# Up projection of an mLSTM + GELU kernel: float32r products of 12-bit parts in place of summed fp32 blocks

## The chip, the cores and the metric

The kernel runs on one core of a Trainium2 chip. The metric is the device time of one execution in microseconds: 517.59 us before the change, the median of three runs (517.13 to 517.72). The profile is one execution of the program as the hardware profiler recorded it; its span from the first to the last instruction is 515.2 us.

## The reference

Two parts follow each other. The first is an mLSTM cell over 4 batches, 8 heads, 768 steps and head size 40, written as a recurrence over time:

```python
for t in range(S):
    m_new = np.maximum(f_gate[:, :, t] + m, i_gate[:, :, t])
    f_stab = np.exp(f_gate[:, :, t] + m - m_new)
    i_stab = np.exp(i_gate[:, :, t] - m_new)
    C = f_stab * C + i_stab * outer(v_t, k_t)
    n = f_stab * n + i_stab * k_t
    y[:, :, t] = sigmoid(o_gate_t) * (C @ q_t) / max(abs(n . q_t), 1)
```

The second takes x, which is y with the heads laid side by side (3072 tokens x 320), and computes `out = gelu(x @ w_in) @ w_out` with the exact gelu, w_in of 320 x 2048 and w_out of 2048 x 320. The two weights arrive as float64 and the result is float32, so x @ w_in has to be computed to about fp32's accuracy.

## The kernel before

**Stages.** The sequence is cut into six chunks of 128 steps; a chunk of all four batches is 512 tokens. For each chunk c and batch b a *cell* (n = 4c + b) turns q and k (`turn`, letter T), makes the decay weights (`mask` M, `weights` W), multiplies them by the scores (`scores` S), takes the part carried from earlier chunks (`carry` C), applies them to v (`values` V), divides (`finish` Y) and turns the result so that features lie on partitions (`turn_y`, X). When the four X of a chunk are done, its *up* (x @ w_in and gelu) can run, and then its *down* (times w_out). The down of chunk c is interleaved with the cells of chunk c + 1 by hand: the string FRONT gives the order for the start (cells of chunks 0 and 1, conversion of the weights from float64 in 26 pieces by K and J, the whole up and down of chunk 0 as A, U and F), and the string DOWN gives it for the down of every later chunk but the last; F is one step of the down, Z a piece of preparation for the weights. The order within an engine's queue is the order in which these letters are played. There are no planner's choices.

**Up before.** For chunks 1 to 5, `summed_up` (products at L597, rest at L626) computes the first 256 features of the contraction as a product of 2 x 2 blocks with seven block products instead of eight (Strassen's form, in Winograd's variant). Rows of x^T are one pair of blocks, halves of the 2048 columns the other, halves of the 512 tokens the third. Each block product is eight fp32 matmuls of 128 x 128 weights with 256 columns. It needs sums of weight blocks (`in_sum`, Z in FRONT, DVE), sums of x blocks (`sum_x`, L587, DVE), and sums of the products, which DVE makes from PSUM into the tile g (L608 to L612 and L639, 512 elements a partition). The remaining 64 features are plain products of half height (`rest`, L626), whose two halves use the two halves of TensorE's rows side by side. gelu follows on ACT (L637, L640), and `hidden_sums` (L525 to L527, DVE) forms the sums that the down needs, since the down too uses seven products (`down_steps`, L682).

**PSUM.** Eight banks in four pairs, with the tags tr, h, a and b. An up takes one bank of each pair for its four result blocks, so that two sets alternate.

**Cell data.** Each of q, k, v and the output gate has four buffers (NLD = 4) and is loaded for cell n + 4 after `turn_y` of cell n. The running maxima M of a cell, 512 KB spread over all partitions, come by DMA from a scratch tensor in memory into two tiles of their own (`Mb`, NM = 2); POOL masks them (L334), ACT makes the weights W from them (L359) in another four tiles. The 64 last features of y are doubled within the gate's tile (L460), so that the third transpose of `turn_y` (L470) yields them on both halves of the partitions.

Of the kernel before, what the change touches and what calls it, by code (L numbers as in the profile page):

```python
# [9 lines left out]
F32 = mybir.dt.float32  # L10
BF16 = mybir.dt.bfloat16
# [4 lines left out]
P = 128  # L16

I23 = 2.0 ** 23

# [6 lines left out]
    O0 L0 I1 I1 g0 E L1 P0 O2 P1 w0 t0 N D K w1 L2 P2 Q P3 s0 O1 t1 w2 L3 c0 J K v0 K s1 y0 w3 t2 I3 g1 v1 O3 I2 I3  # L26
    I5 J c1 B5 I2 K y1 I4 I2 s2 x0 O4 L4 t3 J x1 B4 s3 v2 I7 g3 L5 g2 c2 c3 y2 v3 x2 O5 L6 K J G0 A y3 x3 J H M0 M1
    K K J T0 W0 O6 M2 O7 A J W1 S0 C0 K J T1 L7 U U K Z K V0 T2 A M3 J J G1 S1 K W2 W3 K C1 Z A S2 Z V1 G2 J Y0 J K
    C2 Z T3 J K Y1 U U J S3 Z V2 C3 K J K K J J F K F F F Z J K J X0 K K J F F F Z J F K G3 Y2 F J K V3 J K F K X1 J
    J F F F F K Z X2 B8 J F Y3 X3 B9 F"""  # L30
DOWN = """
    M0 Z M1 T0 W0 F F T1 W1 Z G3 Z F S0 Z S1 C0 M2 Z C1 G1 G0 M3 V0 Y0 Z V1 W2 Z F F T2 W3 F T3 F G2 Z Y1 S2 S3 C2
# [4 lines left out]
def kernel(  # L37
# [19 lines left out]
    L = P  # L57
# [12 lines left out]
    NM = 2  # L70
    NB = 4
    WP = 512
    assert S % L == 0 and 3 * BH <= P and DFF % (4 * WP) == 0 and DM == NX * P + R and DM <= WP and D <= DP and NLD == B == 4

    const = ctx.enter_context(tc.tile_pool(name="const", bufs=1))
    wts = ctx.enter_context(tc.tile_pool(name="wts", bufs=B))
    raw = ctx.enter_context(tc.tile_pool(name="raw", bufs=2))
    two = ctx.enter_context(tc.tile_pool(name="two", bufs=2))
    outp = ctx.enter_context(tc.tile_pool(name="outp", bufs=2))
    dram = ctx.enter_context(tc.tile_pool(name="dram", bufs=1, space=bass.MemoryType.DRAM))  # L80
# [10 lines left out]

    w_in = const.tile([P, NX, 2, DFF // 2], F32, name="w_in")
    w_rest = const.tile([P, DFF // 2], F32, name="w_rest")
# [4 lines left out]
    xT = const.tile([P, NX + 1, TG], F32, name="xT")  # L98
# [5 lines left out]
    qb = [const.tile([P, H, DP], F32, name=f"qb{n}") for n in range(NLD)]  # L104
    kb = [const.tile([P, H, DP], F32, name=f"kb{n}") for n in range(NLD)]
    vb = [const.tile([P, H, D1], F32, name=f"vb{n}") for n in range(NLD)]

    ob = [const.tile([P, DM + R], F32, name=f"ob{n}") for n in range(NLD)]
# [7 lines left out]
    def out_of(n):  # L116
        return ob[n % NLD][:, 0:DM].rearrange("p (h d) -> p h d", d=D)

    def load(n, first=0, end=4):

        if n >= NCH * B:
            return
        c, b = divmod(n, B)
        for src, dst in ((q, qb), (k, kb), (v, vb), (o_gate, None))[first:end]:
            nc.sync.dma_start(out=dst[n % NLD][:, :, 0:D] if dst else out_of(n),
                              in_=src[b, :, c * L:(c + 1) * L, :].rearrange("h p d -> p h d"))
# [3 lines left out]
    def load_M(n):  # L130

        if n >= NCH * B:
            return
        c, b = divmod(n, B)
        Mb[n] = wts.tile([P, H, L], F32, name="Mb", tag="Mb", bufs=NM)
# [5 lines left out]
    for t in kb[0:B] + qb[0:B]:  # L141
        nc.gpsimd.memset(t[:, :, D:DP], 0.0)
    for t in vb[0:B]:
        nc.gpsimd.memset(t[:, :, D:D1], 1.0)
# [106 lines left out]
    for f in range(0, DFF // 2, WP // 2):  # L251
        for x in range(NX):
            pieces.append(([w_src["in"][x * P:(x + 1) * P, w_cols(e, f, WP // 2)] for e in range(2)],
                           w_in[:, x, :, f:f + WP // 2]))
        if f % WP == 0:
            pieces.append(([w_src["in"][NX * P:DM, w_cols(e, f, WP)] for e in range(2)], w_rest[:, f:f + WP]))
    n_in = len(pieces)
# [34 lines left out]
    def conv_two(i):  # L292

        if i < len(pieces):
# [5 lines left out]
            if len(dst.shape) == 3:  # L300
                s, p = [t.rearrange("p (e f) -> p e f", e=2) for t in (s, p)]
# [20 lines left out]
    class Cell:  # L322


        def __init__(self, c):
            self.c = c

            self.engine = nc.vector if c < 2 else nc.gpsimd
            self.qT, self.kT, self.vw, self.far, self.hs = {}, {}, {}, {}, {}
# [7 lines left out]
        def weights(self, b):  # L337

            n = self.c * B + b
            W[n] = wts.tile([P, H, L], F32, name="W", tag="W")  # L340
            if self.c > 0:
                M_n = Mb.pop(n)
# [17 lines left out]
            if self.c > 0 and not 2 * B <= n + NM < 2 * B + NM:  # L360
                load_M(n + NM)

        def gate(self, b):
            o = ob[(self.c * B + b) % NLD][:, 0:DM]
            nc.scalar.activation(out=o, in_=o, func=AF.Sigmoid)

        def turn(self, b):
            n = self.c * B + b
            for src, store, name in ((kb, self.kT, "kT"), (qb, self.qT, "qT")):
                pt = ps_tr.tile([P, NP, L], F32, name="pt", tag="tr")  # L370
                unread(pt[:, 0, :])
                for p in range(NP):
                    nc.tensor.transpose(pt[:, p, :], src[n % NLD][:, 2 * p:2 * p + 2, :].rearrange("p h d -> p (h d)"),  # L373
# [6 lines left out]
        def weigh_values(self, b):  # L380
            vw = self.vw[b] = two.tile([P, H, D1], F32, name="vw", tag="vw")
            self.engine.tensor_tensor(out=vw, in0=vb[(self.c * B + b) % NLD],
# [17 lines left out]
        def carry(self, b):  # L400
# [9 lines left out]
            if c + 1 < NCH:  # L410
                vw = self.vw.pop(b)
                for p in range(NP):
                    for hip in range(2):
                        nc.tensor.matmul(pc[halves[hip], p, :], kb[n % NLD][:, 2 * p + hip, :], vw[:, 2 * p + hip, :],  # L414
                                         start=True, stop=True)
            if c > 0:
# [4 lines left out]
                self.far[b] = two.tile([P, H, D1], F32, name="far", tag="far")  # L421
# [12 lines left out]

        def values(self, b):
# [6 lines left out]
            for h in range(H):  # L442
                for r in halves:
                    nc.tensor.matmul(ph[r, h, :], Pm[:, h, r], vb[n % NLD][:, h, :], start=True, stop=True)  # L444
# [3 lines left out]
            hs = self.hs[b] = two.tile([P, H, D1], F32, name="hs", tag="hs")  # L448
            nc.vector.tensor_tensor(out=hs, in0=ph, in1=self.far.pop(b), op=OP.add)

        def finish(self, b):
            n, hs = self.c * B + b, self.hs.pop(b)
            ys, y = ob[n % NLD], out_of(n)
            self.engine.tensor_tensor(out=y, in0=hs[:, :, 0:D], in1=y, op=OP.mult)
            den = two.tile([P, H], F32, name="den", tag="den")
# [343 lines left out]
```

## Time and profile before

| stretch of the span (us) | what runs | length | TensorE busy | DVE busy | ACT busy |
|---|---|---|---|---|---|
| 0 to 57.5 | cells of chunk 0, first weights | 57.5 | 45.9 | 46.0 | 43.6 |
| 57.5 to 96.0 | cells of chunk 1, up of chunk 0 | 38.5 | 38.4 | 33.0 | 36.1 |
| 96.0 to 133.2 | down of chunk 0, w_out converted | 37.2 | 37.2 | 32.7 | 18.3 |
| 133.2 to 164.9 | up of chunk 1 | 31.7 | 31.7 | 21.9 | 11.0 |
| 164.9 to 212.8 | down of chunk 1, cells of chunk 2 | 47.9 | 47.9 | 35.3 | 25.1 |
| 449.6 to 481.3 | up of chunk 5 | 31.7 | 31.7 | 18.7 | 10.5 |
| 481.3 to 515.2 | down of chunk 5 | 33.9 | 30.7 | 10.6 | 3.3 |

Chunks 2 to 4 repeat the two rows of chunk 1, with ups of 31.6 to 31.7 us. Over the whole span TensorE is busy for 500.3 us (97%), DVE for 340.2 (66%), ACT for 255.0 (49%) and POOL for 60.9 (12%). The granted TensorE clock is 0.992 of full speed on average. A busy engine in such a table need not be the bound: whether it is follows from which wait ends last in the stage, and for that the chain of waits has to be read.

### The profile page before, as it was taken

To read this page: it belongs to the slowest core of one execution; us is meant where nothing else is said; L and a number is where in the kernel's file an instruction comes from. 1 tells how busy PE (TensorE), PEld (TensorE's weight loads), DVE (VectorE), ACT (ScalarE), POOL (GpSimd) and SP (SyncE) were. 2 spreads that over 40 slices of the span, in tenths; PEclk is the share of its full clock that TensorE was granted. 3 is DMA by queue.
4 is the path that set the end of the run, shared out by engine and by line. 5 is a ranking of instruction groups with operands and counts; after the bars stand their busy time and mean duration, and the time that the engine had idled before them with its cause. 6 is when DMAs were issued, how large, how long until landed. Compare 5 with 4: busy or idle time off the path is not lost.

```text
span 515.2 us, 10957 instructions
## 1 busy us (share of the span) xinstructions
PE 500.3 (97%) x4472; PEld 450.6 (87%) x4472; DVE 340.2 (66%) x696; ACT 255.0 (49%) x523; POOL 60.9 (12%) x98
## 2 busy tenths in 40 slices
PE   4889999999999999999999999999999999999997
PEld 3778888767888999988999988999988999988997
DVE  7789598999577887347668347678347657237621
ACT  7696999555344960152980132982123882124300
POOL 3002100000210225000145000053000021000000
PEclk9799999999999999999999999999999999999999
DMA  6999751279900254900234900124920020000001
GB/s 128 223 214 212 184 147 53 64 163 171 198 0 1 84 116 58 167 0 2 74 88 69 167 28 1 43 83 81 166 52 2 5 80 1 27 27 0 1 2 51
DMA packets 111442, 41.62 MB, mean 81 GB/s; under 512 B 101184, under 2 KB 104416, under 8 KB 111392
## 3 DMA queue, kind: packets, MB, share of 16 engines
q1 hardware_dynamic: 111392, 40.92, 37.5%
q8 instruction: 35, 0.57, 0.5%
q14 instruction: 15, 0.12, 0.1%
HBM read 36.90 MB, written 4.01 MB: 79 GB/s over the span
## 4 chain that ended last, share of the span: by engine, by line
PE 91%; ACT 4%; DVE 3%; issue 0%; DMA 0%; SPq 0%; DVEq 0%; ACTq 0%
PE po L682 30%; PE pu L597 24%; PE pu L626 7%; PE po L659 7%; PE pu L538 5%; PE ps L395 4%; PE ph L444 4%; PE pt L373 4%; PE pf L419 2%; PE pf L414 2%; PE pu L544 1%; PE px L470 1%; ACT W L359 1%; ACT pow L285 1%; ACT pow L286 1%; DVE M L194 1%
## 5 line engine op out<-in xcount | busy, mean ns | idle before, releaser
L682 PE MATMUL po<-w_out,g 128*128 128x160 f32 x640 | 91.5, 299 | 0.0
L682 PEld LDWEIGHTS po<-w_out,g 128*128 128x128 f32 x640 | 88.0, 190 | 0.3 <-DVE g L639 0.3
L597 PE MATMUL pu<-xT,w_in 128*128 128x256 f32 x240 | 58.8, 381 | 0.0
L639 DVE TENSOR_TENSOR g<-pu,g 128x512 f32<-128x512 f32 x60 | 40.5, 689 | 22.4 <-PE pu L626 21.0
L597 PEld LDWEIGHTS pu<-xT,w_in 128*128 128x128 f32 x240 | 45.0, 190 | 7.5 <-ACT g L640 1.7
L471 ACT COPY xT<-px 128x384 f32<-128x384 f32 x24 | 11.1, 480 | 77.9 <-PE px L470 77.8
L359 ACT ACTIVATE W<-Mb,aT 128x128 f32<-128x128 f32 x160 | 48.9, 391 | 0.1
L682 PE MATMUL po<-w_sums,sums 128*128 128x160 f32 x320 | 47.3, 302 | 0.0
L398 DVE TENSOR_TENSOR W<-ps,W 128x512 f32<-128x512 f32 x48 | 30.2, 683 | 23.9 <-PE ps L395 21.2
L334 POOL TENSOR_SCALAR_AFFINE_SELECT Mb<-Mb 128x1024 f32<-128x1024 f32 x20 | 22.9, 1155 | 185.3 <-DMA Mb<-M_d 131.2
L682 PEld LDWEIGHTS po<-w_sums,sums 128*128 128x128 f32 x320 | 44.0, 190 | 0.4
L606 ACT COPY g<-pu 128x512 f32<-128x512 f32 x20 | 11.6, 582 | 58.2 <-PE pu L597 58.2
L695 DVE TENSOR_TENSOR o_sb<-po,o_sb 128x320 f32<-128x320 f32 (+1 forms) x27 | 12.5, 463 | 39.4 <-PE po L682 36.2
L637 ACT ACTIVATE g<-pu 128x512 f32<-128x512 f32 x20 | 12.0, 598 | 52.7 <-PE pu L626 52.7
L597 PE MATMUL pu<-x_sums,in_sums 128*128 128x256 f32 x160 | 37.8, 379 | 0.0
L626 PE MATMUL pu<-xT,w_rest 64*128 64x256 f32 x320 | 37.2, 382 | 0.0
L640 ACT ACTIVATE g<-g 128x512 f32<-128x512 f32 x60 | 36.1, 627 | 1.9
L608 DVE TENSOR_TENSOR g<-pu,g 128x512 f32<-128x512 f32 x20 | 13.8, 692 | 34.6 <-PE pu L597 28.8
L626 PEld LDWEIGHTS pu<-xT,w_rest 64*128 64x128 f32 x320 | 30.1, 187 | 6.4 <-issue 3.3
L659 PE MATMUL po<-w_out,g 128*128 128x320 f32 x128 | 35.7, 434 | 0.0
L597 PEld LDWEIGHTS pu<-x_sums,in_sums 128*128 128x128 f32 x160 | 30.2, 190 | 4.3
L659 PEld LDWEIGHTS po<-w_out,g 128*128 128x128 f32 x128 | 23.8, 190 | 9.3
(140 smaller groups left out, 884.3 us busy)
## 6 DMA issues: line engine op xcount, KB each, us to landing
Mb<-M_d SPq DMA_DIRECT2D x20, 512.0 KB, 3.7
bits<-in_moe_w_in_dram SPq DMA_DIRECT2D x20, 256.0 KB, 4.6
bits<-in_moe_w_out_dram SPq DMA_DIRECT2D x16, 320.0 KB, 3.0
vb<-in_v_dram SPq DMA_DIRECT2D x24, 160.0 KB, 4.9
ob<-in_o_gate_dram SPq DMA_DIRECT2D x24, 160.0 KB, 4.2
qb<-in_q_dram SPq DMA_DIRECT2D x24, 160.0 KB, 4.0
kb<-in_k_dram SPq DMA_DIRECT2D x24, 160.0 KB, 4.5
out_dram<-o_sb SPq DMA_DIRECT2D x24, 160.0 KB, 3.0
```

What stands on the lines that cost most here:

```text
L334: nc.gpsimd.affine_select(out=t, in_=t, compare_op=OP.is_ge, fill=1.0e30, base=0, pattern=[[0, H], [1, L]], channel_multiplier=-1)
L359: nc.scalar.activation(out=W[n][:, h, :], in_=src, func=AF.Exp, scale=-1.0, bias=aT[:, self.c, r:r + 1])
L373: nc.tensor.transpose(pt[:, p, :], src[n % NLD][:, 2 * p:2 * p + 2, :].rearrange("p h d -> p (h d)"), ident)
L395: nc.tensor.matmul(ps[hip][:, p, :], kT[r, p, :], qT[r, p, :], start=True, stop=True)
L398: nc.vector.tensor_tensor(out=w, in0=ps[hip], in1=w, op=OP.mult)
L538: nc.tensor.matmul(banks[-1][e][:, i - i0, :], w_in[:, x, e, i * P:(i + 1) * P], xT[:, x, t0:t1], start=(x == 0 and i == i0), stop=False, ...
L597: nc.tensor.matmul(to[:, j, :], lhs[:, (f0 + j) * P:(f0 + j + 1) * P], rhs, start=(first and j == 0), stop=(last and j == 1), skip_group_c ...
L626: nc.tensor.matmul(pair[e][:, j, :], w_rest[halves[e], (f0 + j) * P:(f0 + j + 1) * P], xT[halves[e], NX, HT * h:HT * (h + 1)], start=False ...
L639: nc.vector.tensor_tensor(out=blk[e][h], in0=x, in1=y, op=OP.add),
L640: nc.scalar.activation(out=blk[e][h], in_=blk[e][h], func=AF.Gelu))
L659: nc.tensor.matmul(po[b], g.t[:, f, b * L:(b + 1) * L], w_out[:, f, :], start=(f == 0), stop=(f == NF - 1))
L682: nc.tensor.matmul(bank[at][:, i, :], lhs(j, t), rhs(j), start=(first and i == 0 and j == 0), stop=(i == n - 1 and j == HF - 1), skip_grou ...
```

## The change

For chunks 1 to 5 the seven fp32 block products give way to three products of another kind. The type float32r holds a float32 that TensorE multiplies in a mode of its own[...]. So each weight is split into hi and lo (`split_weight`: ACT makes hi, DVE lo), each x likewise (`split_x`, from PSUM, in `turn_y`), and hi x hi, lo x lo and (hi + lo) x (hi + lo) with suitable factors are summed in PSUM to the full product over a factor of 4097, which gelu's input scale takes back. Each product covers all 512 tokens. The 64 rest features get the same three parts.

One result tile of 128 columns x 512 tokens fills one bank; `up` takes four tiles i of both halves e at a time, so all eight banks are in use, and runs twice. Sum tiles hi + lo of the weights do not fit in SBUF for good and are made again by DVE (`make_all`, `make_rest`) in each chunk, one tile ahead of their use. ACT applies gelu straight from PSUM; no DVE additions lie between. For chunk 0 the up stays as it was, out of the unsplit weights; the splitting begins in FRONT (Z, now `split_in`) once chunk 0's up is done, and tiles 5 to 7 are split within chunk 1's up.

To make room in SBUF, W and M of a cell share one tile (three in all, NW = 3), q, k and v have three buffers (NQ = 3) and are loaded for cell n + 3 when both `carry` and `values` of cell n are through (`read`), M for cell n + 3 after `values` of cell n, `far` and `hs` are one tile, and the doubled 64 features have a single buffer `y_rest`, filled by `twice`. In FRONT and DOWN, loads that now follow from `read` drop out, and M3, W3 and the Z move.

```diff
-    w_in = const.tile([P, NX, 2, DFF // 2], F32, name="w_in")
-    w_rest = const.tile([P, DFF // 2], F32, name="w_rest")
-    xT = const.tile([P, NX + 1, TG], F32, name="xT")
+    x_all, x_lo = [const.tile([P, NX + 1, TG], F32R, name=name) for name in ("x_all", "x_lo")]
...
-        Mb[n] = wts.tile([P, H, L], F32, name="Mb", tag="Mb", bufs=NM)
+        Mb[n] = wts.tile([P, H, L], F32, name="W", tag="W")
...
+        def read(self, b):
+
+            self.reads.append(b)
+            if self.reads.count(b) == 2:
+                load(self.c * B + b + NQ, 0, 3)
...
+            load_M(n + NW)
+            self.read(b)
...
+        def twice(self, b):
+            nc.vector.tensor_copy(out=y_rest, in_=ob[(self.c * B + b) % NLD][:, NX * P:].unsqueeze(1).to_broadcast([P, 2, R]))
...
-            if self.c > 0 and b == B - 1:
-                sum_x()
+            split_x(px, t)
+            load(n + NLD, 3, 4)
...
+    def split_weight(w, hi, lo):
+        nc.scalar.activation(out=hi, in_=w, func=AF.Copy, scale=PART * 2.0 ** -12)
+        nc.vector.scalar_tensor_tensor(out=lo, in0=hi, scalar=-BASE * 2.0 ** 12, in1=w, op0=OP.mult, op1=OP.add)
...
+    def split_x(px, t):
...
+        hi = parts["x"][:, :, t]
+        nc.scalar.activation(out=hi, in_=px, func=AF.Copy, scale=PART)
+        nc.vector.tensor_tensor(out=x_all[:, :, t], in0=px, in1=hi, op=OP.subtract)
+        nc.vector.scalar_tensor_tensor(out=x_lo[:, :, t], in0=px, scalar=-1.0 / BASE, in1=hi, op0=OP.mult, op1=OP.add)
...
+    def make_all(i):
+        if i < HF and i not in all_:
+            while i not in in_lo:
+                split_in(len(in_lo))
+            all_[i] = raw.tile([P, NX, 2, P], F32R, name="in_all", tag="pow") if i % 2 else tile_in(F32R)
+            both(all_[i], parts["in"][i], in_lo[i])
...
+    def up(g):
+
+        def main(i):
+
+            pu = [pool.tile([P, TG], F32, name="pu", tag=tag) for pool, tag in
+                  (((ps_tr, "tr"),) * 2, ((ps_h, "h"),) * 2, ((ps_mm, "a"),) * 2, ((ps_mm, "b"),) * 2)[i % 4]]
+            make_all(i)
+            make_all(i + 1)
+            w = (parts["in"][i], in_lo[i], all_.pop(i))
+            for e in range(2):
+                for n, x in enumerate((parts["x"], x_lo, x_all)):
+                    for j in range(NX):
+                        nc.tensor.matmul(pu[e], w[n][:, j, e, :], x[:, j, :], start=(n == 0 and j == 0), stop=False,
+                                         skip_group_check=True)
+            return pu
+
+        def rest(i, pu):
+            u, m = i // 4, slice(i % 4 * P, (i % 4 + 1) * P)
+            for n, (w, x) in enumerate(((parts["rest"][u], parts["x"]), (rest_lo[u], x_lo), (all_["rest", u], x_all))):
                 for e in range(2):
...
+                    nc.tensor.matmul(pu[e], w[r, m], x[r, NX, :], start=False, stop=(n == 2), skip_group_check=True)
+
+        def out(i, pu, e):
+            nc.scalar.activation(out=g.t[:, HF * e + i, :], in_=pu[e], func=AF.Gelu, scale=4097.0)
+
+        for u in range(2):
+            tiles = range(4 * u, 4 * u + 4)
+            banks = [main(i) for i in tiles]
+            make_rest(u)
+            for i, pu in zip(tiles, banks):
+                rest(i, pu)
+            todo = [(i, e) for i in range(4) for e in range(2)] if u == 0 else [(i, e) for e in range(2) for i in range(4)]
+            for i, e in todo:
+                out(tiles[i], banks[i], e)
+                if (i, e) in ((1, 1), (3, 1)):
+                    hidden_sums(g, tiles[i] - 1, tiles[i] + 1)
...
-        summed_up(g, weight_sum(2) if c == 1 else [])
+        up(g)
+        if c == 1:
+            for step in weight_sum(2):
+                step()
```

## The prediction

> **What bounds the kernel now.** I read the granted clock first (0.992 of full on the one core, so no throttling to explain), then the chain that ended last, then busy time by stage, then the chain inside one chunk. The page's chain:
>
> ```profile
> PE 91%; ACT 4%; DVE 3%; issue 0%; DMA 0%; SPq 0%; DVEq 0%; ACTq 0%
> PE po L682 30%; PE pu L597 24%; PE pu L626 7%; PE po L659 7%; PE pu L538 5%; PE ps L395 4%; PE ph L444 4%; PE pt L373 4%; PE pf L419 2%; PE pf L414 2%; PE pu L544 1%; PE px L470 1%; ACT W L359 1%; ACT pow L285 1%; ACT pow L286 1%; DVE M L194 1%
> ```
>
> TensorE carries 91% of the path. The two lines that the change rewrites, L597 and L626, are 31% of it. Stretches by engine (length, PE, PE loads, DVE, ACT, POOL busy, clock, DMA share, GB/s) for the second later chunk, up and then down:
>
> ```profile
> 212.80:244.50 31.70, 31.70 (x177) 26.93 (x176) 18.74 (x29) 10.58 (x18) 0.00 (x0) 1.00 0.18 31
> 244.50:292.40 47.90, 47.90 (x589) 47.20 (x590) 30.73 (x61) 25.12 (x58) 14.44 (x20) 1.00 0.47 94
> ```
>
> In an up TensorE has no gap at all, while DVE has 13 us and ACT 21 us to spare. So an up is worth what its matmuls take, and any new wait of TensorE is pure loss. The chain through that chunk (start, length, what):
>
> ```profile
> 210.59 2.18 PE po L682 x16
> 212.77 12.09 PE pu L597 x56
> 224.86 3.65 PE pu L626 x32
> 228.51 12.28 PE pu L597 x56
> 240.79 3.65 PE pu L626 x32
> 244.45 1.02 PE pt L373 x8
> 245.47 4.35 PE po L682 x32
> ```
>
> An up is 12.09 + 3.65 + 12.28 + 3.65 = 31.7 us, five times. One fp32 product stands as two records (56 records for 28 products), each 12.09/56 = 216 ns for 256 columns; a pair of half-height rest records takes 3.65/16 = 228 ns.
>
> **What the Trainium skill says.** "TensorE: Matmul & The Clock Gate", section Back-to-back issue gap: N/2.4 + 2.5 ns warm, 216 ns for 512 columns. The trace agrees for bf16: the 512-column matmul starts at 15.08 and the next one 0.22 us later.
>
> ```profile
> 15.08 0.38 PE L356 MATMUL pm<-beyond,eye 128*128 128x512 bf16 x1
> 15.30 0.39 PE L354 MATMUL pm<-M_parts,row 96*128 96x128 bf16 x4
> ```
>
> An fp32 record takes the same 216 ns for half the columns: two cycles a column, four a product. "Perfetto Trace Analysis", section Engine Utilization, puts "÷2 for FP32_LOW_HIGH" on the output rate, which fits: the halving belongs to the low/high handling of fp32. Same TensorE page, section LDWEIGHTS: 128 columns of weights load in 128/1.2 = 107 ns; the trace's fp32 transposes, 8 in 0.87 us = 109 ns each, agree. "VectorE: DVE Perf Modes", section on the TRN2 errata: fp32 tensor_tensor takes (N+151)/0.96, 691 ns at 512; the trace has 689. No page prices a float32r product, and this trace has none.
>
> **The change part by part.**
>
> *Products.* Removed per chunk: 56 products of 128x256 (112 records, 24.4 us) and 64 rest records (7.3 us). Added: 8 tiles x 2 halves x 3 parts x 2 row blocks = 96 float32r products of 512 columns, and 8 x 3 = 24 pairs of half-height ones. Bounds of the unknown price: one cycle a column (the bf16 row, 216 ns) and two in one record (the fp32 record's rate, 512 x 2/2.4 + 2.5 = 429 ns). I take 216 ns: a 12-bit part has no low half to pass separately, and the halved rate is tied to that. The load (107 ns) fits under it. Pairs: 228 ns, since both the stream and two loads are as long as in today's pair. Sum: 96 x 0.216 + 24 x 0.228 = 20.7 + 5.5 = 26.2 us, against 31.7: **5.5 us a chunk, 27.4 us in five**.
>
> *DVE and ACT in an up.* DVE loses 24 adds of 689 ns between products (16.5 us) and gets 8 sums hi+lo and 2 for the rest at 0.69 (6.9 us); hidden_sums stays, now as four groups of three. ACT loses four copies and 12 gelus out of SBUF, gets 16 gelus out of PSUM in all. Their totals are hidden. Their order isn't, because all eight banks are now filled and freed by ACT alone, and DVE makes the third part just ahead of its use. I follow one chunk with these rows (gelus 2.06/4 = 0.52 apart; a group of three sums 2.0 us):
>
> ```profile
> 94.36 2.06 ACT L548 ACTIVATE g<-pu 128x512 f32<-128x512 f32 x4
> 233.63 0.68 DVE L525 TENSOR_TENSOR sums<-g 128x512 f32<-128x512 f32 x1
> 234.34 0.69 DVE L526 TENSOR_TENSOR sums<-sums,g 128x512 f32<-128x512 f32 x1
> 234.95 0.68 DVE L527 TENSOR_TENSOR g<-g 128x512 f32<-128x512 f32 x1
> ```
>
> 1. Start. The sum for tile 0 stands on DVE behind the last down's add (p4), which ran from 212.81 to 213.30 in this chunk, ending 0.7 us after TensorE went on at 212.6. Sum ready at 1.35; TensorE reaches it after four products, 0.86. Wait 0.5. Splitting x (480 ns on ACT, two DVE operations of (384+151)/0.96 = 557 ns by the page's formula) is done by then, behind the 2.18 us of the last down. In chunk 1 the fifth weight split (0.69) and weight_sum(1) (8 x 0.245 = 2.0) stand ahead too: wait 2.1.
> 2. Middle. The sum for tile 5 stands on DVE behind hidden_sums of tiles 0 to 3, which wait for the eight gelus of the first half. From the first rest product: gelus from 0.93, the eighth done at 5.1, its sums at 7.1, tile 5's at 7.8. TensorE: rests 2.74, tile 4 2.6, four products 0.86 = 6.2. **Wait 1.65**; chunk 1 has a split more: 2.35. Queued behind it are tiles 5 to 7 and every later matmul.
> 3. End. After the last rest (2.74 from its first) come k's transposes (0.44), then q's, which need the bank of tile 4's second half: fifth gelu, 4.03 + 0.1. Wait 0.95. The last chunk has no transposes, but its first down needs a bank of tile 7 (fourth gelu, 3.5): wait 0.85.
>
> Sum: 0.5x4 + 2.1 + 1.65x4 + 2.35 + 0.95x4 + 0.85 = 17.7 us.
>
> *y_rest.* One buffer, refilled by DVE only after the preceding transposes; X2 directly follows X1, so its third transpose waits for a handover and a copy (0.2 + 0.28 less two transposes): 0.4 x 4 = 1.6.
>
> *weight_sum(2)* after chunk 1's up: 2.0 us of DVE ahead of the third product of the down, 0.8 left over.
>
> *W and M in three tiles, q, k, v in three buffers.* No engine time. M, q, k, v of cell n+3 start only after values(n). In a down that is about 8.4 us ahead of T3 (178.3 to 186.8 today), with 512 + 2 x 160 KB to land; landings are 3.7 to 4.5 us alone. I take 0.5 for three downs together. In the front, W3's exponentials (28.23) come after v0's matmuls (done 24.7), and t3's loads start at about 25 for 33.4: nothing to 3; I take 1.
>
> *Front, end.* DVE is 88% busy from 96 to 133. Splitting three x blocks adds 3.2 us ahead of Y3; four in_sums (2.8) vanish before 96, of which 1.4 count (S3's multiply is that late, 95.26 against 93.84); so X3 comes about 1.2 later, of which PE loses 0.8. ACT's splits lie in its idle half.
>
> Total lost: 17.7 + 1.6 + 0.8 + 0.5 + 1 + 0.8 = 22.4 against 27.4 won: -5.0, **512.6 us**.
>
> **The rivals.**
> - *The waits don't show* (DVE and ACT run ahead of my count, or loads and transposes fill the gaps): of 27.4 some 21 remain, 496.5. For: DVE has lost 10 us an up. Against: it is the order, not the sum, that makes the wait.
> - *The weight load binds.* Were a float32r load twice an fp32 one (214 ns), the mains still fit, but a rest pair loads twice, 428 ns: 24 x 0.2 x 5 = +24, **536.6, slower**.
> - *Two cycles a column*, as an fp32 record: 120 x 0.213 x 5 = +128, less the waits of the ups, which longer products hide (17): 623, slower. For: each fp32 record runs so. Against: the price is tied to low/high.
> - *The front loses more*: 1 KB rows in place of 2 KB for the first weights at a DMA share of 0.89 up to 57 us, later q, k, v, DVE full. 8 us more: 520.5, slower.
>
> **How the numbers follow.** Forecast 0.48; no waits 0.16; front 0.16; load 0.10; two cycles 0.06; gain and waits equal, no change, 0.04. The range 497 to 524 holds the forecast, nearly all of the no-wait case and the front case: about 0.8. Faster: 0.46 of the forecast's 0.48 and 0.16 = 0.62. Same: 0.04 + 0.02. Slower: 0.16 + 0.10 + 0.06 = 0.32.
>
> **What would show it.** Product price: starts of the products in the up, 216 or 429 ns apart, and rest pairs of 228. Step 2: TensorE idle before the fifth product of tile 5 (x_all), released by DVE's hi+lo sum, and hidden_sums ahead of that sum on DVE. Step 3: q's transposes waiting for ACT's gelu. y_rest: a px transpose waiting for DVE. Front: the first float32r product starting within 2 us of 133. It is wrong if records come in pairs, if PE waits on DMA in the front, or if an up has no gap.

## The result and the profile after

The changed kernel takes 525.75 us (median of four runs, 524.37 to 526.28) against 517.60 before: a ratio of 1.0158, interval 1.0143 to 1.0172. It is slower by 8.2 us where the forecast was 5 us faster, and it lies above the range. The profiled executions differ by 9.3 us (span 524.5 against 515.2), and the steps below add up to that number.

The chain that ended last, from the page of the changed kernel (L644 and L653 are the products of the new up, L704 and L681 the downs, L656 the gelu, L572 a part of `hidden_sums`):

```profile
PE 72%; DVE 16%; ACT 9%; issue 1%; DMA 0%; SPq 0%; DVEq 0%; ACTq 0%
PE po L704 29%; PE pu L644 17%; PE ps L396 4%; PE pu L653 4%; PE ph L453 3%; PE pu L585 3%; PE pt L374 3%; ACT g L656 3%; PE pf L420 2%; PE pf L415 1%; PE px L487 1%; ACT pow L291 1%; DVE w_out L306 1%; DVE sums L572 1%; ACT pow L292 1%
```

TensorE's share of the path fell from 91% to 72%, and the two lines of the up from 31% to 21%. What took their place is DVE and ACT: TensorE now waits for work that it used to run ahead of. Where, is told by three stretches of the changed kernel (columns as before: length, busy time and number of instructions of PE, PE loads, DVE, ACT and POOL, granted clock, DMA share, GB/s): the first down with the cells of chunk 1, the up of chunk 2, its down.

```profile
97.00:142.00 45.00, 39.91 (x173) 26.68 (x173) 36.91 (x94) 20.14 (x39) 2.71 (x3) 0.96 0.53 121
224.10:254.30 30.20, 29.19 (x148) 22.17 (x146) 10.78 (x17) 5.81 (x11) 0.00 (x0) 1.00 0.04 12
254.30:303.10 48.80, 48.11 (x590) 46.96 (x589) 31.76 (x64) 26.98 (x61) 15.17 (x20) 1.00 0.58 105
```

The kernel before, in the first of these stretches:

```profile
97.00:133.00 36.00, 36.00 (x169) 25.61 (x168) 31.54 (x87) 17.76 (x33) 0.00 (x0) 1.00 0.77 143
```

There TensorE had no gap; now it idles 5 us in 45, and DVE does 5.4 us more. The up of chunk 2 takes 30.2 us, 1.6 less than before, and its down 0.9 to 1.0 more. Read from the starts of the ups (133.03, 212.61, 292.19, 371.77, 449.48 before; 141.96, 224.10, 303.12, 382.44, 459.59 after), the account against the prediction is:

| part | predicted, us | measured, us |
|---|---|---|
| five ups without their waits | -27.4 | -15.6 |
| waits inside the ups | +13.9 | +11.6 |
| downs of chunks 1 to 4 (q's wait, doubled rest, sums, loads) | +6.7 | +4.4 |
| front, to the first product of chunk 1's up | +1.8 | +8.9 |
| sum | -5.0 | +9.3 |

The first row and the second are told apart by an experiment whose ups have no wait in chunks 2 to 4 and take 28.65 us (below): 31.77 - 28.65 = 3.12 us won in each. Two terms carry the miss: the products are worth 11.8 us less than forecast, and the front costs 7.1 us more.

Of the front's 8.9 us, 0.9 lie ahead of chunk 0's up, whose first product starts at 43.45 before and at 44.34 after, and these are not the change's doing. They go with the clock that TensorE got in the first 25 us: a bf16 product of 512 columns at 15.1 us is followed by the next after 0.22 us before the change and after 0.43 us after it. The experiments below share this part of the kernel with the change; those whose profile has the full clock at that place start chunk 0's up between 43.1 and 43.5 us, the others between 43.9 and 44.3, and one, which had half the clock once more at 37.8 us, at 46.0. The other 8.0 us are the first down.

**The waits** are where the prediction put them. The chain through the up of chunk 2 in the changed kernel (start, length, what):

```profile
224.41 0.49 DVE o_sb L717
224.91 0.61 DVE w_in L526
...
225.56 10.48 PE pu L644 x44
236.04 0.94 PE pu L653 x6
236.98 2.06 ACT g L656 x4
239.06 0.70 DVE sums L572
...
242.44 0.60 DVE g L574
243.04 0.61 DVE in_all L526
243.70 7.70 PE pu L644 x32
251.40 3.02 PE pu L653 x24
254.41 1.08 ACT g L656 x2
```

First the start: the last down's add, then tile 0's sum, then TensorE. Then the middle: gelus, six sums of the hidden layer and only then tile 5's sum (L526, `both`), for which TensorE waits. At the end q's transposes wait for a gelu. In TensorE's own timeline of the same up (start, length, instruction, and in brackets its idle time before and who ended it):

```profile
228.91 0.63 PE L644 MATMUL pu<-x_hi,w_in_hi 128*128 128x512 f32 x2
229.38 0.62 PE L644 MATMUL pu<-x_lo,w_in 128*128 128x512 f32 x2
229.84 0.63 PE L644 MATMUL pu<-x_all,in_all 128*128 128x512 f32 x2
...
243.70 0.74 PE L644 MATMUL pu<-x_all,in_all 128*128 128x512 f32 x2 [0.76 <-DVE in_all L526]
244.27 0.63 PE L644 MATMUL pu<-x_hi,w_in_hi 128*128 128x512 f32 x2
...
255.54 0.66 PE L374 MATMUL pt<-ident,qb 128*128 128x128 f32 x4 [0.59 <-ACT g L656]
```

The middle wait leaves TensorE idle for 0.76 us and the first pair behind it takes 0.57 us to the next start instead of 0.465, the end wait is 0.59. And the price stands here too: one pair of products of 512 columns starts 0.465 us after the other, one record for each product: **232 ns a product**, not the 216 that I took. (That the products of the parts add up to fp32's accuracy is what the change counts on; no run here measures the accuracy of a single product.)

**The front** is a ring, and three timelines of the changed kernel show it. TensorE:

```profile
131.34 3.60 PE L681 MATMUL po<-w_out,g 128*128 128x320 f32 x8 [2.41 <-DVE w_out L306]
139.69 0.41 PE L487 MATMUL px<-ident,ob 128*128 128x128 f32 x2 [1.75 <-DVE ob L470]
```

DVE (L543 and L544 are DVE's part of `split_x`, L306 makes a block of w_out):

```profile
129.35 0.56 DVE L543 TENSOR_TENSOR x_all<-px,x_hi 128x384 fp32r<-128x384 f32 x1 [0.74 <-ACT x_hi L542]
129.82 0.55 DVE L544 SCALAR_TENSOR_TENSOR x_lo<-px,x_hi 128x384 fp32r<-128x384 f32 x1
...
130.80 0.49 DVE L306 SCALAR_TENSOR_TENSOR w_out<-sig,pow 128x320 f32<-128x320 f32 x1
...
136.15 0.56 DVE L543 TENSOR_TENSOR x_all<-px,x_hi 128x384 fp32r<-128x384 f32 x1 [2.93 <-ACT x_hi L542]
```

ACT:

```profile
135.63 0.49 ACT L542 ACTIVATE x_hi<-px 128x384 fp32r<-128x384 f32 x1 [1.98 <-PE px L487]
```

Read in order: at 128.6 DVE reaches the split of a block and idles 0.74 us for ACT's copy, which stands behind ACT's part of the conversions. The w_out block that TensorE wants stands behind that split, is done at 131.3, and TensorE, idle for 2.41 us, goes on. Its turn of the next block stands behind those products, so ACT's copy comes at 135.63 and DVE, at the next split, idles 2.93 us, with the division of the last block (`finish`, L470) behind it. For that TensorE waits 1.75 us more. Each engine waits for the next.

The granted clock comes on top of the ring's waits. The same sequence of eight products, three transposes and eight products runs once ahead of the 2.41-us wait and once behind it (columns as above; the clock is the third number from the end):

```profile
118.94:123.84 4.90, 4.90 (x19) 3.24 (x19) 4.65 (x13) 2.89 (x5) 0.00 (x0) 1.00 0.47 134
131.34:137.93 6.59, 6.58 (x19) 4.23 (x19) 3.56 (x9) 1.61 (x3) 0.00 (x0) 0.74 0.16 27
132.43:135.85 3.42, 3.42 (x9) 2.24 (x9) 0.76 (x3) 1.35 (x3) 0.00 (x0) 0.50 0.01 2
```

For 3.4 us, from 1.1 us after TensorE went on, it had half its clock. The profiles of the two kernels below that keep this ring (tile 5's sum first, 256 columns) have such a stretch behind the same wait too; why the clock falls was not tested by itself. Up to the end of the transposes that ACT's copy waits for, this took 4.25 us in place of 2.74: about 1.5 of the front's 8.9 us. Of the four timed runs the one whose mean clock is 0.999 took 524.37 us and the two with 0.997, which is what one such stretch leaves, 526.00 and 526.28; the fourth, at 0.990, took 525.51. A trace is kept of the run of 526.28 alone.

### The profile page after: what moved, and what is told of

Read it like the earlier page. It is cut to its first block, busy times and chain, and to the rows that moved or that the text cites. A ratio compares the mean times of both kernels' runs of the same rounds, so it can differ in the third digit from the quotient of the medians.

```text
span 524.5 us, 10610 instructions
## 1 busy us (share of the span) xinstructions
PE 493.8 (94%) x4312; PEld 426.7 (81%) x4312; DVE 311.5 (59%) x663; ACT 245.1 (47%) x513; POOL 62.4 (12%) x95
## 4 chain that ended last, share of the span: by engine, by line
PE 72%; DVE 16%; ACT 9%; issue 1%; DMA 0%; SPq 0%; DVEq 0%; ACTq 0%
PE po L704 29%; PE pu L644 17%; PE ps L396 4%; PE pu L653 4%; PE ph L453 3%; PE pu L585 3%; PE pt L374 3%; ACT g L656 3%; PE pf L420 2%; PE pf L415 1%; PE px L487 1%; ACT pow L291 1%; DVE w_out L306 1%; DVE sums L572 1%; ACT pow L292 1%
## 5 line engine op out<-in xcount | busy, mean ns | idle before, releaser
L656 ACT ACTIVATE g<-pu 128x512 f32<-128x512 f32 x80 | 41.9, 617 | 121.0 <-PE pu L653 119.6
L704 PE MATMUL po<-w_out,g 128*128 128x160 f32 x640 | 91.5, 299 | 0.7 <-ACT g L656 0.7
L704 PEld LDWEIGHTS po<-w_out,g 128*128 128x128 f32 x640 | 88.2, 190 | 1.1 <-ACT g L656 1.1
L572 DVE TENSOR_TENSOR sums<-g 128x512 f32<-128x512 f32 x20 | 13.8, 690 | 65.4 <-ACT g L656 65.4
L644 PE MATMUL pu<-x_lo,w_in 128*128 128x512 f32 x160 | 50.3, 395 | 1.6 <-DVE w_in L523 1.6
L644 PE MATMUL pu<-x_hi,w_in_hi 128*128 128x512 f32 x160 | 51.6, 403 | 0.0
L362 ACT ACTIVATE W<-W,aT 128x128 f32<-128x128 f32 x160 | 48.9, 391 | 0.1
L704 PE MATMUL po<-w_sums,sums 128*128 128x160 f32 x320 | 47.3, 302 | 0.0
L399 DVE TENSOR_TENSOR W<-ps,W 128x512 f32<-128x512 f32 x48 | 30.2, 683 | 26.6 <-PE ps L396 24.0
L704 PEld LDWEIGHTS po<-w_sums,sums 128*128 128x128 f32 x320 | 44.0, 190 | 0.4
L681 PE MATMUL po<-w_out,g 128*128 128x320 f32 x128 | 38.3, 451 | 3.3 <-DVE w_out L306 3.2
L644 PEld LDWEIGHTS pu<-x_lo,w_in 128*128 128x128 f32 x160 | 29.9, 188 | 9.6 <-DVE w_in L523 2.5
L681 PEld LDWEIGHTS po<-w_out,g 128*128 128x128 f32 x128 | 24.1, 196 | 14.7 <-DVE w_out L306 6.0
L644 PEld LDWEIGHTS pu<-x_hi,w_in_hi 128*128 128x128 f32 x160 | 29.5, 188 | 8.0 <-ACT g L656 1.8
L339 POOL TENSOR_SCALAR_AFFINE_SELECT W<-W 128x1024 f32<-128x1024 f32 x20 | 22.6, 1135 | 98.8 <-DVE den L467 29.6
L585 PE MATMUL pu<-first_x,w_in 128*128 128x256 f32 x128 | 28.8, 381 | 0.5 <-DVE W L399 0.5
L644 PE MATMUL pu<-x_all,in_all 128*128 128x512 f32 x80 | 25.7, 403 | 3.1 <-DVE in_all L526 3.1
L644 PE MATMUL pu<-x_all,w_in 128*128 128x512 f32 x80 | 25.4, 398 | 2.6 <-DVE w_in L526 2.6
L585 PEld LDWEIGHTS pu<-first_x,w_in 128*128 128x128 f32 x128 | 23.8, 190 | 3.8 <-DVE W L399 0.8
```

The costliest lines, as they stand in the source:

```text
L339: nc.gpsimd.affine_select(out=t, in_=t, compare_op=OP.is_ge, fill=1.0e30, base=0, pattern=[[0, H], [1, L]], channel_multiplier=-1)
L362: nc.scalar.activation(out=W[n][:, h, :], in_=src, func=AF.Exp, scale=-1.0, bias=aT[:, self.c, r:r + 1])
L399: nc.vector.tensor_tensor(out=w, in0=ps[hip], in1=w, op=OP.mult)
L572: nc.vector.tensor_tensor(out=s1, in0=a21, in1=a22, op=OP.add)
L585: nc.tensor.matmul(banks[-1][e][:, i - i0, :], w_in[i][:, x, e, :], first_x[:, x, t0:t1], start=(x == 0 and i == i0), stop=False, skip_gro ...
L644: nc.tensor.matmul(pu[e], w[n][:, j, e, :], x[:, j, :], start=(n == 0 and j == 0), stop=False, skip_group_check=True)
```

## The experiments

All but the narrow products were timed in three rounds against the kernel before on the same chip. "First down" below is the time from the first product of chunk 0's down to the first product of chunk 1's up, in the profiled run: 37.1 us before, 45.1 after.

**The buffers alone.** The kernel before, with only the memory part of the change:

```diff
-    qb = [const.tile([P, H, DP], F32, name=f"qb{n}") for n in range(NLD)]
+    qb = [const.tile([P, H, DP], F32, name=f"qb{n}") for n in range(NQ)]
...
-        Mb[n] = wts.tile([P, H, L], F32, name="Mb", tag="Mb", bufs=NM)
+        Mb[n] = wts.tile([P, H, L], F32, name="W", tag="W")
```

> The kernel before with the buffer part of the change alone: W and M in three shared tiles, q, k, v in three buffers loaded after both reads, one y_rest, the moved M3 and W3; products, sums and the Z of before. The trace of the changed kernel has its first float32r product at 141.96 us where the seven-product up began at 133.03, so 8.9 us are lost ahead of it. Theory A (the splitting of x and of the weights in the queues of DVE and ACT loses them, the buffers only the 0.9 us that are already there at the first up product, 44.34 against 43.45): 518.5 us, the first L-up product of chunk 1 at about 134. Theory B (late loads of q, k, v and M and the single y_rest lose them): 525 us or more, chunk 1's up at 140 or later.

519.88 us, ratio 1.0051 (1.0036 to 1.0066), 2.8 us over the kernel before: theory B is out, the buffers don't cost the front's 8 us. The first down takes 37.8 us (+0.7) and each of four chunks 79.90 us in place of 79.58 (+1.3 together). The other 0.8 us stand ahead of chunk 0's up, which starts at 44.26 us, and go with the clock, as said above. Something else moved: the masks of shared tiles now wait for the tile, and with the weighting of v behind them run on GpSimd inside the first down (2.78 us of POOL there, none before). Three of DVE's operations beside them take 0.86 to 1.21 us where others of their kind take 0.32 to 0.49, 1.8 us more in sum.

**The late split of x in the front.** In FRONT, DVE's part of `split_x` for chunk 1 gets a letter R and stands behind conversions of w_out, instead of following ACT's copy at once; DOWN is as in the change:

```diff
-    J F F F F K X2 J F Y3 X3 Z F"""
+    J R R F F F F K X2 J F Y3 R X3 R Z F"""
...
-        nc.vector.tensor_tensor(out=x_all[:, :, t], in0=px, in1=hi, op=OP.subtract)
...
+        if late:
+            late_x.append(rest_of)
+        else:
+            rest_of()
```

> The changed kernel with the two DVE operations of split_x taken out of turn_y in chunk 1 and played later (R in FRONT: the first two just before the last but one X, the third after the last finish, the fourth after the last X); ACT's hi stays. Same work, other place in DVE's queue. Theory A1 (they stand between conversions of w_out and wait for ACT and so for TensorE, which itself waits for the conversions: a ring of waits): chunk 1's up starts 4 to 6 us earlier, 520 to 522 us. Theory A2 (DVE simply has 4.2 us more to do in this stretch, 36.9 against 32.7, and is full): at most 1.5 us, 524 to 526 us.

520.96 us, ratio 1.0072 (1.0056 to 1.0088): 3.8 us over the kernel before in place of 8.2, by order alone, with the same operations. The first down takes 40.8 us, 4.3 less. TensorE's two longest waits there are now these:

```profile
127.64 2.42 PE L690 MATMUL po<-w_out,g 128*128 128x320 f32 x8 [0.64 <-DVE w_out L306]
134.44 0.41 PE L487 MATMUL px<-ident,ob 128*128 128x128 f32 x2 [1.90 <-DVE ob L470]
```

The wait of 2.41 us is gone, and with it the stretch of half clock, so the 4.3 us contain the 1.5 us from above. The ring is shown. Of the 8.0 us that the first down had lost, 3.7 stay.

**No weight splits in the front.** All weight splits are left to the first up that needs them:

```diff
-    C2 T3 J K Y1 U U J S3 Z V2 C3 K J K K J J F K F F F Z J K J X0 K K J F F F Z J F K G3 Y2 F J K V3 J K F K X1 J
+    C2 T3 J K Y1 U U J S3 V2 C3 K J K K J J F K F F F J K J X0 K K J F F F J F K G3 Y2 F J K V3 J K F K X1 J
...
-    J F F F F K X2 J F Y3 X3 Z F"""
+    J F F F F K X2 J F Y3 X3 F"""
```

(The string has four Z, not five: in the changed kernel tiles 0 to 3 are split in the front and 4 to 7 within chunk 1's up.)

> The changed kernel without the five Z (weight splits) in FRONT; all eight tiles are split inside chunk 1's up. Theory A2: the end of the front comes 4 us earlier (six DVE operations of 0.69 us), of which chunk 1's up gives 3 back, total 524 to 525. Theory A1: the ring stays, so the front gains 2 at most and the up gives 3 back: 526 to 527.

526.18 us, ratio 1.0175 (1.0157 to 1.0192), no better than the change itself. In the profile the first down is 1.3 us shorter (43.8) and chunk 1's up 0.4 longer (a stretch of half clock, 135.9 to 139.3 us, lies in this first down too); the times show nothing of it. The weight splits aren't what fills the front.

**Tile 5's sum first.** In an up the sum of tile 5 is queued ahead of `hidden_sums`:

```diff
+            make_all(4 * u + 5)
             todo = [(i, e) for i in range(4) for e in range(2)] if u == 0 else [(i, e) for e in range(2) for i in range(4)]
```

> The changed kernel with the hi+lo sum of the weight tile 5 (in chunk 1 its split too) queued on DVE ahead of hidden_sums of the first half. In the trace TensorE waits for it 0.76 us in every later chunk (idle, and 1.2 us counted from the end of the product ahead). If that wait is the prediction's middle step, it goes and nothing takes its place: 1.0 us a chunk, 520.5 to 521. Rival (hidden_sums, now later, delays the third product of the down or the gelus bind): no more than 1.5 us in all, 524.

523.38 us, ratio 1.0121 (1.0095 to 1.0146). A chunk is 77.98 us long in place of 79.02: 1.04 less, of which 0.76 was TensorE's idle time and 0.1 the slower restart. The time is 2.4 us under the changed kernel's, and not the 5 that were expected: chunk 1's up, where the split of tile 5 was moved as well, grew from 33.3 to 34.9 us: TensorE waits 1.86 us there for the split of tile 6, where the changed kernel waits 1.23 for that of tile 5. The chain through the up of chunk 2 now has no DVE between its halves:

```profile
226.06 10.48 PE pu L644 x44
236.54 2.98 PE pu L653 x24
239.52 11.34 PE pu L644 x48
250.87 3.02 PE pu L653 x24
```

**Products of 256 columns.** It measures the disputed price by itself:

```diff
-                        nc.tensor.matmul(pu[e], w[n][:, j, e, :], x[:, j, :], start=(n == 0 and j == 0), stop=False,
+                        for h in range(2):
+                            t = slice(HT * h, HT * (h + 1))
+                            nc.tensor.matmul(pu[e][:, t], w[n][:, j, e, :], x[:, j, t],
```

> The changed kernel with each main float32r product of 512 columns split into two of 256 (192 instead of 96 a chunk, each with its own weight load, the same multiplications). It measures what sets the 232 ns between two starts of float32r products. Theory P (the stream sets it: one cycle a column, 213 ns, and about 19 ns for each instruction, the load of 107 ns lying under it): 107 + 19 = about 126 ns a product, an up longer by 96 x 0.02 = about 1.9 us, the kernel by 9 us, 535 us. Theory L (the weight load sets it, twice 107 ns and a little): still about 232 ns for half the columns, an up longer by 96 x 0.232 = 22 us, the kernel by 111 us, about 637 us.

TensorE's timeline, four products in a line, each with its own weight load:

```profile
231.01 0.64 PE L646 MATMUL pu<-x_hi,w_in_hi 128*128 128x256 f32 x4
231.49 0.64 PE L646 MATMUL pu<-x_lo,w_in 128*128 128x256 f32 x4
231.96 0.64 PE L646 MATMUL pu<-x_all,w_in 128*128 128x256 f32 x4
```

Four starts take 0.478 us: 119.6 ns for 256 columns against 232.3 for 512. Theory L is out: the time halves with the columns although the loads double. Theory P holds in kind, and its split of the price was wrong: if the stream alone sets both points, they give 0.440 ns a column and about 7 ns for each instruction, not 0.417 and 19 (with two points this can't be told from a load that begins to bind at 256 columns). The up of chunk 2 is 0.5 us longer, the kernel takes 527.08 us in its one run.

**Chunk 1's cell work on GpSimd.** The late-split kernel with one more edit:

```diff
-            self.engine = nc.vector if c < 2 else nc.gpsimd
+            self.engine = nc.vector if c < 1 else nc.gpsimd
```

> The changed kernel with the late split of x, and chunk 1's cell work that later chunks give to GpSimd (gating by the output gate, the state's decay) given to GpSimd too, in place of VectorE. In the late-split kernel the first down and chunk 1's cells still end 3.7 us later than before (up of chunk 1 at 136.8). If what is left there is VectorE's sum of work (theory A2), that up starts 1 to 3 us earlier, at 134 to 136, and the time is 518 to 520 us. If it is the order of waits through the single buffer of the doubled rest (theory A3), nothing changes within 0.5 us (521), or it gets worse because GpSimd is slower per operation and stands in the same chain.

521.92 us, ratio 1.0089 (1.0067 to 1.0112); the first down is 41.1 us, no better than 40.8. That would speak for A3, but DVE's busy time hardly fell: 36.2 us in the stretch from 97 to 137, against 36.5 in the late-split kernel up to 136.8. DVE's timeline tells why:

```profile
123.01 1.21 DVE L289 TENSOR_SCALAR pow<-bits 128x320 uint32<-128x320 uint32 x1
124.14 1.21 DVE L294 TENSOR_SCALAR sig<-bits 128x320 uint32<-128x320 uint32 x1
125.38 0.91 DVE L296 SCALAR_TENSOR_TENSOR sig<-bits,sig 128x320 f32<-128x320 uint32 x1
```

and GpSimd's of the same time:

```profile
121.78 0.96 POOL L465 TENSOR_TENSOR ob<-far,ob 128x320 f32<-128x320 f32 x1 [21.99 <-DVE far L460]
122.70 2.47 POOL L339 TENSOR_SCALAR_AFFINE_SELECT W<-W 128x1024 f32<-128x1024 f32 x2
125.14 1.74 POOL L383 TENSOR_TENSOR vw<-vb,ewT 128x328 f32<-128x328 f32 x2
```

While GpSimd runs, operations that take DVE 0.32 us elsewhere (L289, L294) take 1.21. The Trainium skill says in "SBUF — State Buffer", section "SBUF: two separate sides", that the two share a pair of ports and that, for some of their operations, whoever starts first holds it and "the other fully blocks"; the trace agrees in direction, with 0.32 against 1.21 us. Over the first down such longer operations add 3.5 us to DVE's time here and 1.7 in the late-split kernel, about what the four operations that left DVE had taken. So this run could not tell A2 from A3, and two more were made.

**A doubled rest for each block of chunk 1**, in the late-split kernel, in memory of `w_sums` that is free at that time:

```diff
+        def rest_of(self, b):
+            if self.c == 1:
+                return w_sums[1][:, b, 0:2 * R].rearrange("p (two r) -> p two r", r=R)
+            return y_rest
```

> The late-split kernel, and each block of chunk 1 keeps its doubled rest in a place of its own (memory of a later sum that is still free there) instead of waiting for the single buffer, as blocks had it in the kernel before. If the 3.7 us that the front still lacks stand in the order of waits through that buffer (theory A3: 1.9 us on a finish's last multiplication, 0.8 on the doubled rest), the up of chunk 1 starts 1 to 2.7 us earlier, at 134 to 135.8, and the time is 518 to 520 us against 520.96. If it is VectorE's sum of work (theory A2: busy 36.5 of 39.8 us there, against 31.5 of 36.0 before), nothing is won: within 0.5 us.

521.50 us, ratio 1.0073 (1.0052 to 1.0095), first down 40.6 us: 0.2 us won. The single buffer isn't what holds the front; A3 falls.

**Less work for DVE.** The late-split kernel without the operation that ors the sign into w_out, whose weights are then all without their signs; only its time is used:

```diff
-            nc.vector.scalar_tensor_tensor(out=pu, in0=hi, scalar=0x80000000, in1=pu,
-                                           op0=OP.bitwise_and, op1=OP.bitwise_or)
+            if pieces[i][1].shape[1] != DM:
+                nc.vector.scalar_tensor_tensor(out=pu, in0=hi, scalar=0x80000000, in1=pu,
+                                               op0=OP.bitwise_and, op1=OP.bitwise_or)
```

> The late-split kernel without the sign of the second weights: VectorE's operation that ors the sign bit in (0.48 us) is left out for the 16 pieces of w_out, 12 of them between 97 and 137 us, 5.8 us of VectorE's work. Nothing else is changed. If VectorE's sum of work holds the front (theory A2), TensorE loses its idle time there (2.6 us) and the up of chunk 1 starts at about 134, the time 518 us. If an order of waits through the single buffer or ScalarE holds it (theory A3), the start stays within 0.7 us of 136.8 and the time at 521.

517.15 us, ratio 0.9997 (0.9985 to 1.0008); the first down is 36.9 us, 3.9 less and as long as before the change. The stretches of the late-split kernel and of this one:

```profile
97.00:136.80 39.80, 37.15 (x171) 25.04 (x169) 36.50 (x93) 19.12 (x37) 2.99 (x3) 1.00 0.59 130
```

```profile
97.00:132.70 35.70, 35.70 (x168) 25.43 (x167) 29.56 (x79) 18.90 (x36) 2.78 (x3) 1.00 0.61 141
```

With DVE busy for 29.6 of 35.7 us, and not for 36.5 of 39.8, TensorE has no gap. A2 is shown: once the ring is open, what remains in the front is the sum of DVE's work. The edit also shortens the way of each w_out block by an operation, but the late-split profile fits a full queue: from 112.9 us to the end of the division that TensorE waits for, at 134.3, DVE has one idle time of more than 0.11 us, of 0.46.

**Four orders mended.** The late split, tile 5's sum first, the sums of tiles 0 and 1 ahead of the last part of the preceding down (letter B), and the gelus of tile 4 first in an up's second half:

```diff
+    J R R F F F F K X2 J F Y3 R X3 R Z B F"""
...
+            make_all(4 * u + 5)
+            todo = [(i, e) for i in range(4) for e in range(2)]
+            if u == 1:
+                todo = [(0, 0), (0, 1), (1, 0), (2, 0), (3, 0), (1, 1), (2, 1), (3, 1)]
```

> The changed kernel with four orders mended: the late split of x in the front; the sum of tile 5 ahead of hidden_sums in an up; the sums of tiles 0 and 1 queued ahead of the last part of the preceding down; and the gelus of an up's second half in the order tile 4 first half, tile 4 second half, then as before. Nothing is left out or added. If the waits are what this theory says they are, they add: 525.75 - 5.0 (front) - 2.4 (middle) - 0.4 x 5 (start, c1 more) - 0.5 x 4 (end) = 514 us (512 to 516), faster than the kernel before (517.1). A rival is that removing one wait only lets the next begin earlier (ACT's gelus alone set when banks come free): then 518 to 521.

514.11 us, ratio 0.9931 (0.9904 to 0.9958): faster than both, and the total that the waits counted one by one had given. In the profile their shares differ: the front gives 2.8 us for 5.0, because chunk 0's up starts at 46.04 us there, the ends of the downs give 3.5 for 2.0. The up of chunk 2 and its down:

```profile
221.50:250.15 28.65, 28.65 (x147) 22.31 (x145) 10.46 (x17) 6.00 (x12) 0.00 (x0) 1.00 0.04 13
250.15:298.20 48.05, 47.95 (x591) 47.03 (x589) 33.03 (x65) 26.58 (x60) 15.18 (x20) 1.00 0.56 106
```

No gap is left in the up, so its 28.65 us are what the products cost. The count of instructions at 232 ns gives 96 x 0.2323 + 24 x 0.2315 = 27.86. The other 0.8 stands at the handovers, in TensorE's timeline:

```profile
232.31 0.62 PE L653 MATMUL pu<-x_all,in_all 128*128 128x512 f32 x2
232.86 0.50 PE L662 MATMUL pu<-x_hi,w_rest_hi 64*128 64x512 f32 x2
233.19 0.40 PE L662 MATMUL pu<-x_lo,w_rest 64*128 64x512 f32 x2
233.42 0.41 PE L662 MATMUL pu<-x_all,w_rest 64*128 64x512 f32 x2
```

The last two full products take 0.55 us up to the first half-height pair instead of 0.465, and that pair takes 0.33 instead of 0.23. About 0.1 us goes at each of eight such places in an up. Why, no run here tells. In chunk 1 nothing was won, its up even grew from 33.3 to 34.4 us: TensorE waits there for weight splits (1.9 and 0.4 us), and behind the longer of these waits it has half its clock from 164.07 to 167.48 us, in which a pair of products takes 0.85 us in place of 0.465.

**The same with chunk 1's cell work on GpSimd**, the two edits together:

> The kernel with four orders mended, and chunk 1's cell work that later chunks give to GpSimd on GpSimd as well. If VectorE's sum of work is what is left in the front: 1 to 3 us under the kernel with four orders alone (511 to 514). If not: equal to it within 0.5 us, or slower.

512.98 us, ratio 0.9912 (0.9896 to 0.9929). The interval overlaps that of the kernel without the GpSimd part, its first down is no shorter (41.0 against 40.6 us), and in the profiles its chunk 0's up starts 2.1 us earlier (43.92 against 46.04), ahead of all that was changed; so the 1.1 us between the medians are not shown to be its doing.

**And with a doubled rest for each block of chunk 1:**

> The kernel with four orders mended and chunk 1's cell work on GpSimd, and each block of chunk 1 with a doubled rest of its own. Theory A3: 1 to 2.7 us below 512.98, so 510.3 to 512. Theory A2: 512.98 within 0.5 us.

512.70 us, ratio 0.9919 (0.9889 to 0.9949): equal to the one ahead of it, as A2 has it. These two are the fastest versions found, 4.6 to 5.1 us under the kernel before.

## Why the prediction was wrong

**Products, the largest miss.** The step "I take 216 ns" took the bf16 row's price for float32r. It came to 232 (27.86 us an up for 26.2: 1.7 in each, 8.3 in five), and 0.8 us of handovers in each up were not foreseen at all (4 us). One record a product and no halved rate were right, so *two cycles a column* is out by far; *the weight load binds* is out too, since a pair of half-height products, which loads twice, still takes 232 ns. The formula in "TensorE: Matmul & The Clock Gate" of the Trainium skill (section Back-to-back issue gap), which the page gives for a single matmul in isolation, makes 216 ns for 512 columns and 109 for 256; float32r shows 232 and 120, so the measurement decides. The bound from above that I kept, 429 ns, was much too far off to be of use; a price just above the bf16 one never entered the range.

**Waits.** Mechanism and place were right at all three, and in chunks 2 to 4 the waits were together a quarter shorter than forecast: middle 1.04 us for 1.65 (by the run with tile 5's sum first), start 0.5 for 0.5 (what is left of 30.20 - 28.65), end 0.8 for 0.95 (the downs with four orders mended, 48.03 for 48.82). In chunk 1 start and middle were 4.7 us together for 4.45. That the middle wait came out shorter follows from the mis-sized price: TensorE's side of that race, 6.2 us in the prediction, is 2.78 + 2.79 + 0.93 and three handovers of 0.1, so 6.8, and the wait 0.6 shorter. *The waits don't show* was wrong.

**Downs.** With the end wait gone a down takes 48.03 us and 47.81 before the change, so 0.2 us are all that is left for the doubled rest, for which 0.4 stood. `weight_sum(2)` shows nothing (48.82 us in chunk 1, 48.83 in chunk 2), nor do T3's loads.

**Front.** The step that failed is "Splitting three x blocks adds 3.2 us ahead of Y3 ... of which PE loses 0.8". I counted DVE's work and not its waits. `split_x` on DVE waits for ACT, ACT for a transpose, the transpose stands behind products that wait for w_out, and w_out stands behind the split: 4.3 us, shown by moving the split, and about 1.5 us of it the half clock behind the ring's longest wait. The clock had no term: I had read its mean for the kernel before and set it aside. A further 3.7 us are DVE's sum of work, shown by taking work away; buffers alone account for 0.7 of it. DVE was busy 31.5 of 36.0 us there, and the prediction itself had read "DVE is 88% busy": that leaves 4.5 us of room, where the splits of four blocks bring 8 operations 0.47 us apart, 3.8 us, and GpSimd's masks, which the buffers moved to that time, lengthen DVE's operations as well (by 1.7 us of the 36.5 in the late-split kernel; how much of the 3.7 us is theirs was not measured). The remaining 0.9 us belong to the two profiled runs and not to the change. The rival *The front loses more* was near in size, 8 us for the 7.1 by which the front exceeded the forecast. Of its three causes only the last, a full DVE, was one: DMA is 0% of the path.

**The sum.** Without the front's loss the kernel would be about level with the one before: the gain of 15.6 us against waits and downs of 16.0. That the change can win at all is shown by the mended orders.

## What to carry to other kernels

On an engine with 12% of room, don't add only the durations: look for what a new operation waits for and what stands behind it in the same queue, since a ring through three engines cost more than the work itself. And look at the clock of the stretch behind a long TensorE wait, not only at its mean: here the wait's price did not end with the wait. When a tightly packed matmul stream gets a new data type, its price is a term multiplied by every instruction (600 here), so 7% of doubt about it belongs in the range. And queue the operand of the next matmul ahead of anything that waits for results of this one: that single line was worth 1 us in each of chunks 2 to 5, though in chunk 1, where more work came with it, it cost 1.6.

## What the runs showed of the hardware

- A float32r product of 128 x 128 weights is one record and costs 232 ns at 512 columns and 120 at 256, each with a weight load of its own; an fp32 product of 256 columns is two records of 216 ns.
- Two half-height float32r products side by side cost as much as one of full height, 232 ns.
- Going over from full-height to half-height float32r products, or back, cost about 0.1 us on either side: 0.8 us in an up of 28.65.
- With GpSimd at work, DVE's operations of 0.32 us took up to 1.21 us, so moving work to GpSimd did not relieve DVE.
- Half the clock for 3.4 us came 3.4 to 3.6 us after the beginning of each of the three TensorE waits of 2.41 us (the changed kernel, tile 5's sum first, 256 columns). Of the waits of 1.9 to 2.1 us some were followed by such a stretch (no weight splits in the front, four orders mended) and some were not (late split, doubled rests).
